# Unpadded attention tiles, two weight conversions before the first tile's outputs, and the sign cast of sixteen blocks on GpSimd

## The chip, the core and the metric

The kernel runs on one core of a Trainium2 chip. The metric is device microseconds (us) of one execution; the number quoted is a median of three. Engines: TensorE (PE; its weight loads are PEld), VectorE (DVE), ScalarE (ACT), GpSimd (POOL), and SyncE (SP), which here only issues transfers. Each engine works through its own instructions in the order in which the program gives them.

## What is computed

A recurrent attention of batch 4, 8 heads, 768 positions and head size 48 is followed by two feed-forward layers with gates:

```
y[t]  = r[t] @ (state + u * k[t] v[t]^T);   state = w * state + k[t] v[t]^T
h     = max(x @ w1, x @ w2, x @ w3);        x2 = h @ w_out
xn    = rms_norm(x2) * g
out   = (silu(xn @ w_gate) * (xn @ w_val)) @ w_out2
```

x has 3072 rows of 384; the first layer is 768 wide, the second 1536. All inputs are float32, and the products are made from a high and a low part of each operand (three matmuls for one).

## The kernel before

Attention. The 768 positions are cut into 6 chunks of 128, for 4 batches each: 24 tiles. For a tile i, `load_tile` (L251) queues four transfers on SP: two halves of `raw` (r and k transposed, 48 partitions each, L258), r and k as 128 rows (`tm`, L260), and v as 128 rows (L261). `raw` has three buffers of [128, 2, 514], `tm` three buffers whose parts r, k and v begin at elements 0, 386 and 770 (`KO`, `VO`); so the 514, 386 and 770 leave gaps of two elements behind rows of 512, 384 and 768. `load_next` issues one queued transfer. `prep` multiplies `raw` by powers of the decay (L316, DVE) and makes `ru` = r * u * k (L324, L325; DVE for the first eight tiles). `prep_b` sums `ru` by heads (L332, DVE) and puts the sums on diagonals, `Dg` (L335, POOL). `prep2` scales k (L343, POOL). `pe_a` makes the masked scores `pa` of a tile on PE (L352), `mix` merges them into `Dg` (L359, DVE), `pe_y` makes the outputs `py` (L410, PE), `fin` splits these into high and low x (L425 ACT, L426 DVE), and `pe_st` makes the state update (L378 PE, L365 ACT, and from the second chunk on L384 and L386 on POOL).

Weights. They arrive as 64-bit words and are converted into float32 in 60 blocks of 128x384, numbered by `jobs`: 0 to 17 for the first layer's three inputs, 18 to 23 for its output, the rest for the second layer. One `tick` (L221) advances a conversion pipeline by a step: with a counter i it issues the load of block i+3 (`conv_load`, L124, SP; five buffers `wraw`), the three ACT instructions of block i+1 (`conv_exp`: L137 scales the high word, L139 writes the 16 low bits of each element, L140 casts to float16 and so writes sign and exponent into the 16 high bits), the merge of block i on DVE (`conv_shift`, L147), and the split of block i-1 (`conv_put`, `w_split`: high part on ACT, L155; the low part, L156, is put off until after the next step of the program, on POOL, or on DVE for blocks 2, 16, 19 and 22).

Order. It is written out by hand. The part before the loop makes decay tables, loads tiles 0 to 2, does `prep` of tiles 0 and 1 and `pe_a(0)`, and calls `tick` twice, which only issues the loads of blocks 0 and 1. Then six steps are run one after another, each followed by the put-off work, one transfer and one `tick` (L619): `block(0)`, `ahead(2)`, `ahead_b(2)`, `block(1)`, `ahead(3)`, `ahead_b(3)`. `block(i)` is `pe_a(i+1)`, `mix(i+1)`, `pe_y(i)`, `fin(i)`, `pe_st(i)` and the queuing of tile i+3; `ahead` is `prep` with two transfers, `ahead_b` is `prep_b` and `prep2`. After that the first feed-forward layer runs in slots of nine matmuls (`a_l1`, L99 to L101, then L492, L495, L497 and L498 on ACT, DVE and POOL), with the remaining attention steps and the ticks (`U0T`) between the slots. The low part of the first layer's x and h goes to POOL where a slot has 256 columns. The first wide stretch of matmuls begins there; all of the second layer comes after 400 us.

Of the kernel before, what the change touches and what calls it, by code (L numbers as in the profile page):

```python
# [9 lines left out]
F32 = mybir.dt.float32  # L10
# [8 lines left out]
DRAM = bass.MemoryType.DRAM  # L19

B, H, S, D = 4, 8, 768, 48
KO = 386
VO = 770

# [2 lines left out]
RMS_EARLY = 2  # L29
WARM = 24  # L30
TKI = (0, 0, 2)
TKP = (1, 1, 1, 1, 1, 1)
HF = 2
U0T = (1, 1, 1, 1, 0, 1, 1, 1, 0, 1, 1, 1, 1, 1, 1, 0, 1, 1, 1, 0, 1, 1, 1, 1, 1, 1, 1, 1, 1, 1)
LEAD = 4

# [24 lines left out]
NP = H // 2  # L63
# [8 lines left out]
def rwkv_moe_kernel(ctx, tc, rkT, rkv, wd, ub, cst, rg, w1p, wo1p, w2p, out):  # L72
# [59 lines left out]
    def conv_exp(n):  # L132
        if n - 6 >= conv_put.job:
            sums_step(99)
        w = cw[n] = cp.tile([128, CW], F32, tag="wf", bufs=6, name=f"wf{n}")
        lo, hi = conv_words(n)
        act.activation(w, hi.bitcast(F32), AF.Copy, scale=2.0 ** -112)  # L137
        x = cbits(n).rearrange("p (n two) -> p n two", two=2)
        act.activation(x[:, :, 0], lo, AF.Copy, scale=2.0 ** -29 * (1 - 2.0 ** -12), bias=-0.4996)  # L139
        act.activation(x[:, :, 1].bitcast(F16), w, AF.Copy)  # L140

    def cbits(n):
        return craw[n].bitcast(U16)[:, 0:2 * CW]
# [77 lines left out]
    def tick(n=1):  # L221
        for _ in range(n):
            i = tick_n[0]
            tick_n[0] += 1
            for off, fn in ((3, conv_load), (1, conv_exp), (0, conv_shift), (-1, conv_put)):
                if 0 <= i + off < NJ:
                    fn(i + off)
# [10 lines left out]
    kt = tp.tile([128, DM], F32, name="kt")  # L238
    Tst = [tp.tile([128, NP, 96], F32, name=f"T{b}") for b in range(B)]

    raws = [tp.tile([128, 2, 514], F32, name=f"raw{n}") for n in range(3)]


    raw_t, tm_t, loads = {}, {}, []
# [1 line left out]
    def load_next(n=1):  # L246
        for _ in range(n):
            if loads:
                loads.pop(0)()

    def load_tile(i):  # L251
        if i >= NT:
            return
        a = raws[i % 3][:, :, 0:512].rearrange("p s (q t) -> p s q t", t=128)
        t = tp.tile([128, VO + NP * 144], F32, tag="tm", bufs=3, name=f"tm{i}")
        raw_t[i], tm_t[i] = a, t
        for j in range(2):
            loads.append(lambda j=j: sync.dma_start(a[64 * j:64 * j + 48], rkT[i, 48 * j:48 * j + 48]))  # L258
        rk = t[:, 0:2 * KO].rearrange("p (s n) -> p s n", s=2)[:, :, 0:DM]
        loads.append(lambda: sync.dma_start(rk, rkv[i, :, 0:2 * DM].rearrange("p (s n) -> p s n", s=2)))  # L260
        loads.append(lambda: sync.dma_start(t[:, VO:], rkv[i, :, 2 * DM:]))  # L261

    def tables():
        p = ap_.tile([128, NP, 65], F32, tag="h1h", name="ptab")
# [53 lines left out]
    def prep(i):  # L318
        prep_raw(i)
        s = st[i]  # L320
        tm = s["tm"]
        ru = tp.tile([128, DM], F32, tag="ru", name=f"ru{i}")
        eng = dve if i < NRU else pool
        eng.tensor_tensor(out=ru, in0=tm[:, 0:DM], in1=usb, op=ALU.mult)  # L324
        eng.tensor_tensor(out=ru, in0=ru, in1=tm[:, KO:KO + DM], op=ALU.mult)  # L325
        s["ru"] = ru

    def prep_b(i):
        s = st[i]
        a8 = tp.tile([128, H], F32, tag="a8", bufs=2, name=f"a8{i}")  # L330
        ru = s["ru"]
        dve.tensor_reduce(out=a8, in_=ru.rearrange("p (h d) -> p h d", d=D), op=ALU.add,  # L332
                          axis=mybir.AxisListType.X)
        Dg = tp.tile([128, H, 128], F32, tag="Dg", bufs=2, name=f"Dg{i}")
        pool.affine_select(out=Dg, in_=a8.unsqueeze(2).to_broadcast([128, H, 128]),  # L335
                           pattern=[[0, H], [1, 128]], channel_multiplier=-1, base=0,
                           compare_op=ALU.is_equal, fill=0.0)
        s["Dg"] = Dg

    def prep2(i):  # L340
        if i // B < NB - 1:
            k = st[i]["tm"][:, KO:KO + DM]
            pool.tensor_tensor(out=k, in0=k, in1=kt, op=ALU.mult)  # L343

    def pe_a(i):
# [9 lines left out]
    def mix(i):  # L355
        s = st[i]
        dg = s["Dg"].rearrange("p (r j) t -> p r j t", j=2)
        for j in range(2):
            dve.copy_predicated(out=dg[:, :, j], mask=cmask.unsqueeze(1).to_broadcast([128, NP, 128]),  # L359
                                data=s["pa"][j])  # L360
# [6 lines left out]
    def pe_st(i):  # L367
        s = st[i]
        c, b = divmod(i, B)
        if c == NB - 1:  # L370
            return
        tm = s["tm"]
        v3 = tm[:, VO:].rearrange("p (r q e) -> p r q e", q=3, e=D)
        pk = psx.tile([128, NP, D], F32, tag="x", name=f"pkv{i}")
        for pr in range(NP):
            for j in range(2):
                o = KO + 96 * pr + 48 * j
                pe.matmul(pk[64 * j:64 * j + 64, pr], tm[:, o:o + 64], v3[:, pr, 2 * j], start=True, stop=True)  # L378
        if c == 0:
            mask_kv(Tst[b], pk)  # L380
        else:
            kv = tp.tile([128, NP, 96], F32, tag="kv", name=f"kv{i}")
            mask_kv(kv, pk)
            pool.tensor_tensor(out=Tst[b], in0=Tst[b],  # L384
                               in1=w128.unsqueeze(2).to_broadcast([128, NP, 96]), op=ALU.mult)
            pool.tensor_tensor(out=Tst[b], in0=Tst[b], in1=kv, op=ALU.add)  # L386
# [190 lines left out]
    with tc.manual_schedule():  # L577
# [36 lines left out]
        prep(1)  # L614
        load_tile(2)
        load_next(4)
        prep_b(1)
        prep2(1)
        while pos < 6:  # L619
            steps[pos]()  # L620
            flush()
            pos += 1
            load_next()
            tick(TKP[pos - 1])

# [513 lines left out]
        def recurrence():  # L1139

            TB = 8
            wf = gp.tile([96, NP], F32, name="g_w")
            uf = gp.tile([96, NP], F32, name="g_u")
            m2 = gp.tile([96, 2], F32, name="g_m")
            sync.dma_start(wf, wd)
            sync.dma_start(uf, ub.rearrange("(r p) -> p r", p=96))
            sync.dma_start(m2, cst[0:96, 256:258])
            state = gp.tile([96, B, NP, D], F32, name="g_state")
            dve.memset(state, 0.0)

            def wide(a):
                return a.unsqueeze(1).unsqueeze(3).to_broadcast([96, B, NP, D])

            with tc.For_i(0, NB) as c, tc.For_i(0, 128, TB) as t0:
                rk = gp.tile([96, B, 2, NP, TB], F32, tag="g_rk", name="g_rk")
                for b in range(B):
                    for s in range(2):
                        sync.dma_start(rk[:, b, s], rkT[bass.ds(c * B + b, 1), :, s, :, bass.ds(t0, TB)].squeeze(0))
                py = psx.tile([D, B, NP, 2, TB], F32, tag="x", name="g_py")
                for t in range(TB):  # L1160
                    v = gp.tile([96, B, NP, D], F32, tag="g_v", bufs=3, name=f"g_v{t}")
                    for b in range(B):
                        row = rkv[bass.ds(c * B + b, 1), bass.ds(t0 + t, 1), 2 * DM:].rearrange(
                            "a o (r q e) -> (a o) r q e", q=3, e=D)
                        for j in range(2):
                            sync.dma_start(v[48 * j:48 * j + 48, b],
                                           row[0, :, 2 * j].partition_broadcast(48))
                    r, k = (rk[:, :, s, :, t:t + 1].to_broadcast([96, B, NP, D]) for s in range(2))
                    cur = gp.tile([96, B, NP, D], F32, tag="g_cur", bufs=2, name=f"g_cur{t}")
                    dve.tensor_tensor(out=v, in0=v, in1=k, op=ALU.mult)  # L1170
                    dve.tensor_tensor(out=cur, in0=v, in1=wide(uf), op=ALU.mult)
                    dve.tensor_tensor(out=cur, in0=cur, in1=state, op=ALU.add)
                    dve.tensor_tensor(out=cur, in0=cur, in1=r, op=ALU.mult)
                    dve.tensor_tensor(out=state, in0=state, in1=wide(wf), op=ALU.mult)
                    dve.tensor_tensor(out=state, in0=state, in1=v, op=ALU.add)
                    for b in range(B):
                        for pr in range(NP):
                            pe.matmul(py[:, b, pr, :, t], cur[:, b, pr], m2, start=True, stop=True)
                ys = gp.tile([D, B, NP, 2, TB], F32, tag="g_ys", bufs=2, name="g_ys")
                act.copy(ys, py)  # L1180
                for b in range(B):
                    dst = yd[bass.ds(c, 1), :, b, bass.ds(t0, TB)].squeeze(0)
                    sync.dma_start(dst.rearrange("(r e) t -> e r t", e=D),
                                   ys[:, b].rearrange("e r j t -> e (r j) t"))
# [128 lines left out]
```

## Time and profile before

| what | us |
|---|---|
| median of 3 runs (814.71 to 815.89) | 815.61 |
| the profiled execution | 816.15 |
| its span, first to last instruction | 814.4 |
| PE busy in the span | 793.0 |
| DVE, ACT, POOL busy | 578.6, 427.3, 241.1 |

The profiled execution is 0.54 us above the median, and 1.75 us of it lie around the span. PE is busy for 97% of the span. A row of the timeline reads: start in us, duration in us, engine, line, operation, tile written from tiles read, sizes, count; in brackets the idle time of the engine ahead of it and what ended that. "issue" stands for a wait that the profile can't name.

### The profile page before, as it was taken

Reading aid. Unit: us, or ns where it says so; the run is one execution under the profiler, and the core shown is the slowest. Engines: PE = TensorE matmul, PEld = TensorE weight load, DVE = VectorE, ACT = ScalarE, POOL = GpSimd, SP = SyncE. Lnnn points to the kernel's source line nnn. Section 1 sums busy time; section 2 is a strip of 40 time slices with the busy share of each in tenths; the row PEclk is TensorE's granted clock in tenths of the full one; section 3 lists DMA queues with packets and bytes.
Section 4 is the critical chain, followed back from the end, with each engine's and each line's share of the span. In section 5 each row is a group of like instructions: output and inputs, shape, how many; then the busy total and the mean of one; then the engine's idle time right before and its main releaser. Section 6 shows DMA issues by size and latency. Waiting matters only on the chain.

```text
span 814.4 us, 14091 instructions
## 1 busy us (share of the span) xinstructions
PE 793.0 (97%) x5098; PEld 652.2 (80%) x5098; DVE 578.6 (71%) x948; ACT 427.3 (52%) x812; POOL 241.1 (30%) x241
## 2 busy tenths in 40 slices
PE   7799999999999999999999999999999999999996
PEld 6688887888888888888787888788888788888884
DVE  8898979948959748518946679866677884665551
ACT  1998865455453542224576666555444555444431
POOL 2488834544354541013267773000000000000000
PEclk8999999999999999999999999999999999999999
DMA  9996685666475654035279874318454405544211
GB/s 240 272 271 187 222 251 179 187 218 206 136 236 160 211 188 147 20 130 165 87 247 331 282 238 169 118 57 278 139 183 145 130 26 175 157 153 141 73 40 43
DMA packets 83594, 139.28 MB, mean 171 GB/s; under 512 B 10550, under 2 KB 46902, under 8 KB 83516
## 3 DMA queue, kind: packets, MB, share of 16 engines
q1 hardware_dynamic: 80172, 122.37, 48.9%
q0 software_dynamic: 3200, 15.73, 5.1%
q8 instruction: 42, 0.69, 0.4%
q14 instruction: 36, 0.29, 0.1%
q10 hardware_dynamic: 144, 0.20, 0.1%
HBM read 98.65 MB, written 35.41 MB: 165 GB/s over the span
## 4 chain that ended last, share of the span: by engine, by line
PE 84%; DVE 6%; DMA 3%; ACT 3%; issue 2%; SPq 0%; POOL 0%; DVEq 0%; ACTq 0%; POOLq 0%
PE px L99 11%; PE px L100 11%; PE px L101 11%; PE pl L99 8%; PE pl L101 7%; PE pl L100 7%; PE pa L100 5%; PE pa L101 5%; PE pa L99 5%; PE py L410 4%; PE po L100 3%; PE po L99 3%; PE po L101 3%; PE pa L352 2%; DMA raw<-in_rkT 1%
## 5 line engine op out<-in xcount | busy, mean ns | idle before, releaser
L99 PE MATMUL pl<-x,w_a 128*128 128x512 f32 (+1 forms) x342 | 132.0, 386 | 1.4 <-DVE c L495 1.0
L100 PE MATMUL pl<-x,w_a 128*128 128x512 f32 (+1 forms) x342 | 129.6, 379 | 0.7 <-DVE x L426 0.7
L101 PE MATMUL pl<-x,w_a 128*128 128x512 f32 (+1 forms) x342 | 129.6, 379 | 0.5 <-POOL w_a L156 0.5
L99 PEld LDWEIGHTS pl<-x,w_a 128*128 128x128 f32 x342 | 64.3, 188 | 15.0 <-DVE c L495 1.4
L101 PEld LDWEIGHTS pl<-x,w_a 128*128 128x128 f32 x342 | 64.3, 188 | 13.0 <-POOL w_a L156 0.7
L100 PEld LDWEIGHTS pl<-x,w_a 128*128 128x128 f32 x342 | 64.4, 188 | 12.6 <-DVE x L426 1.1
L495 DVE TENSOR_TENSOR c<-pl,c 128x512 f32<-128x512 f32 (+1 forms) x76 | 49.9, 657 | 28.8 <-PE pl L101 26.6
L1031 DVE TENSOR_TENSOR px<-px,sb 128x512 f32<-128x512 f32 x56 | 39.0, 698 | 33.0 <-PE px L101 32.1
L497 ACT CAST h1h<-c 128x512 fp32r<-128x512 f32 (+1 forms) x32 | 19.0, 594 | 82.1 <-DVE c L495 82.0
L147 DVE SCALAR_TENSOR_TENSOR wf<-wf,wraw 128x384 uint32<-128x384 uint32 x60 | 46.3, 775 | 13.1 <-ACT wraw L140 12.6
L335 POOL TENSOR_SCALAR_AFFINE_SELECT Dg<-a 128x1024 f32<-128x1024 f32 x24 | 30.2, 1259 | 80.2 <-DVE a L332 67.2
L1019 ACT COPY sb<-px 128x512 f32<-128x512 f32 x63 | 37.0, 587 | 32.0 <-PE px L101 28.3
L657 POOL TENSOR_TENSOR ws<-wsf,ws 128x384 fp32r<-128x384 f32 x40 | 41.7, 1042 | 40.1 <-ACT ws L656 29.9
L100 PE MATMUL px<-hb,wo 128*128 128x512 f32 x132 | 51.6, 391 | 0.2 <-DVE hb L1017 0.2
L99 PE MATMUL px<-hb,wo 128*128 128x512 f32 x132 | 51.6, 391 | 0.0
L101 PE MATMUL px<-hb,wo 128*128 128x512 f32 x132 | 51.4, 390 | 0.0
L359 DVE COPY_PREDICATED Dg<-csb,pa 128x512 f32<-128x512 uint32 x48 | 32.5, 731 | 20.3 <-PE pa L352 17.1
L410 PE MATMUL py<-Dg,tm 128*32 128x128 f32 x768 | 40.6, 288 | 0.0
L1055 DVE TENSOR_TENSOR hb<-h,hb 128x512 fp32r<-128x512 f32 x36 | 24.9, 691 | 21.8 <-ACT hb L1054 21.6
L139 ACT ACTIVATE wraw<-wraw 128x384 uint16<-128x384 uint32 x60 | 38.9, 648 | 2.0
L140 ACT ACTIVATE wraw<-wf 128x384 f16<-128x384 f32 x60 | 38.7, 645 | 2.0
L137 ACT ACTIVATE wf<-wraw 128x384 f32<-128x384 f32 x60 | 33.5, 558 | 11.2 <-DMA w2o<-wf 10.1
(306 smaller groups left out, 2116.5 us busy)
## 6 DMA issues: line engine op xcount, KB each, us to landing
ws<-w2s SPq DMA_DIRECT2D x80, 384.0 KB, 3.0
w2s<-ws POOLq DMA_DIRECT2D x40, 384.0 KB, 3.5
wraw<-in_w2p SPq DMA_DIRECT2D x36, 384.0 KB, 5.1
raw<-in_rkT SPq DMA_DIRECT2D x48, 192.0 KB, 3.6
tm<-in_rkv SPq DMA_DIRECT2D x24, 384.0 KB, 4.1
wsf<-w2f SPq DMA_DIRECT2D x120, 64.0 KB, 3.2
tm<-in_rkv SPq DMA_DIRECT2D x24, 288.0 KB, 4.4
wraw<-in_w1p SPq DMA_DIRECT2D x18, 384.0 KB, 7.9
```

The costliest lines, as they stand in the source:

```text
L99: pe.matmul(o, lh, rh, start=start, stop=False, **kw)
L100: pe.matmul(o, lh, rl, start=False, stop=False, **kw)
L101: pe.matmul(o, ll, rh, start=False, stop=stop, **kw)
L137: act.activation(w, hi.bitcast(F32), AF.Copy, scale=2.0 ** -112)
L139: act.activation(x[:, :, 0], lo, AF.Copy, scale=2.0 ** -29 * (1 - 2.0 ** -12), bias=-0.4996)
L140: act.activation(x[:, :, 1].bitcast(F16), w, AF.Copy)
L147: dve.scalar_tensor_tensor(out=wu, in0=wu, scalar=3, in1=cbits(n).bitcast(U32), op0=ALU.logical_shift_left, op1=ALU.bitwise_or)
L410: pe.matmul(o, l, r, start=start, stop=stop)
L495: dve.tensor_tensor(out=c1[:, :n], in0=p[:, :n], in1=c1[:, :n], op=ALU.max)
L657: pool.tensor_tensor(out=t[:, :, 1], in0=r, in1=r32(t[:, :, 0]), op=ALU.subtract)
L1019: (act.copy if kind == "e" else dve.tensor_copy)(get(ks[1]), get(ks[0]))
L1031: dve.tensor_tensor(out=o, in0=a, in1=b, op=op)
```

## The change

The tiles lose their gaps: `raw` becomes [128, 2, 4, 128], the parts of `tm` begin at 0, 384 and 768, and r and k come as one row of 768 elements instead of two of 384. Two ticks are moved up: the first stands behind the loads of tile 2, the second behind `mix(1)`, with `block(0)` written out around it; the ticks of the loop then begin with `ahead(2)`. From there on every tick does a block one higher than before at the same place in the program. For blocks 2 to 17 the cast to float16 is issued on POOL instead of ACT.

```diff
-KO = 386
-VO = 770
+VO = 768
-TKP = (1, 1, 1, 1, 1, 1)
+TKP = (0, 1, 1, 1, 1, 1)
+POOL_S = tuple(range(2, 18))
...
-        act.activation(x[:, :, 1].bitcast(F16), w, AF.Copy)
+        if n in POOL_S:
+            pool.tensor_copy(x[:, :, 1].bitcast(F16), w)
+        else:
+            act.activation(x[:, :, 1].bitcast(F16), w, AF.Copy)
...
-    raws = [tp.tile([128, 2, 514], F32, name=f"raw{n}") for n in range(3)]
+    raws = [tp.tile([128, 2, NP, 128], F32, name=f"raw{n}") for n in range(3)]
...
-        a = raws[i % 3][:, :, 0:512].rearrange("p s (q t) -> p s q t", t=128)
+        a = raws[i % 3]
...
-        rk = t[:, 0:2 * KO].rearrange("p (s n) -> p s n", s=2)[:, :, 0:DM]
-        loads.append(lambda: sync.dma_start(rk, rkv[i, :, 0:2 * DM].rearrange("p (s n) -> p s n", s=2)))
-        loads.append(lambda: sync.dma_start(t[:, VO:], rkv[i, :, 2 * DM:]))
+        loads.append(lambda: sync.dma_start(t[:, 0:VO], rkv[i, :, 0:VO]))
+        loads.append(lambda: sync.dma_start(t[:, VO:], rkv[i, :, VO:]))
...
         prep(1)
         load_tile(2)
         load_next(4)
+        tick()
         prep_b(1)
         prep2(1)
+        pe_a(1)
+        mix(1)
+        tick()
+        pe_y(0)
+        fin(0)
+        pe_st(0)
+        load_tile(3)
+        pos = 1
+        load_next()
         while pos < 6:
```

The other lines replace `KO` by `DM` where k is read.

## Rows read from the trace of the kernel before

**Rows 1.** Windows: length, busy us (count) of PE, PEld, DVE, ACT, POOL; clock, DMA
```profile
20.00:40.00 20.00, 15.63 (x213) 13.31 (x216) 17.13 (x27) 18.91 (x39) 8.76 (x8) 0.91 1.00 270
40.00:60.00 20.00, 18.36 (x215) 16.59 (x208) 18.19 (x28) 19.33 (x42) 16.97 (x15) 1.00 0.93 266
60.00:80.00 20.00, 20.00 (x230) 16.58 (x230) 17.55 (x27) 16.24 (x34) 16.17 (x15) 1.00 0.65 198
```

**Rows 2.** Timeline of PE: starts of the tiles' scores, and the wait near 128 us
```profile
29.76 1.25 PE L352 MATMUL pa<-raw 48*128 48x128 f32 x16 [0.49 <-PE pl L101]
...
38.39 1.25 PE L352 MATMUL pa<-raw 48*128 48x128 f32 x16 [1.14 <-issue]
...
49.43 1.25 PE L352 MATMUL pa<-raw 48*128 48x128 f32 x16 [1.03 <-issue]
...
60.84 1.16 PE L352 MATMUL pa<-raw 48*128 48x128 f32 x16
...
73.01 1.16 PE L352 MATMUL pa<-raw 48*128 48x128 f32 x16
...
128.53 0.50 PE L99 MATMUL pl<-x,w_a 128*128 128x512 f32 x1 [0.98 <-DVE c L495]
```

**Rows 3.** Timeline of ACT: first output, a wait for a load, one sign cast
```profile
20.05 0.48 ACT L425 CAST x<-py 128x384 fp32r<-128x384 f32 x1 [5.83 <-PE py L410]
...
28.41 0.56 ACT L137 ACTIVATE wf<-wraw 128x384 f32<-128x384 f32 x1 [0.39 <-DMA wraw<-in_w1p]
...
48.51 0.63 ACT L140 ACTIVATE wraw<-wf 128x384 f16<-128x384 f32 x1
```

**Rows 4.** Timeline of SP and the transfers' sums of 0 to 70 us
```profile
20.70 0.38 SPq L260 DMA_DIRECT2D tm<-in_rkv  x1
...
22.31 0.91 SPq L124 DMA_DIRECT2D wraw<-in_w1p  x2
...
q1 hardware_dynamic: 9042, 17.41, 90.2%
```

**Rows 5.** Timeline of DVE: products of raw, ru, merges, and two waits for ACT
```profile
28.44 1.21 DVE L316 TENSOR_TENSOR raw<-raw,qk 128x1024 f32<-128x1024 f32 x1
...
32.87 0.64 DVE L156 TENSOR_TENSOR w_a<-wf,w_a 128x384 fp32r<-128x384 f32 x1 [1.22 <-ACT w_a L155]
...
39.96 0.55 DVE L147 SCALAR_TENSOR_TENSOR wf<-wf,wraw 128x384 uint32<-128x384 uint32 x1
...
47.28 2.04 DVE L316 TENSOR_TENSOR raw<-raw,qk 128x1024 f32<-128x1024 f32 x1
...
56.96 1.53 DVE L316 TENSOR_TENSOR raw<-raw,qk 128x1024 f32<-128x1024 f32 x1
...
64.77 0.79 DVE L147 SCALAR_TENSOR_TENSOR wf<-wf,wraw 128x384 uint32<-128x384 uint32 x1 [1.41 <-ACT wraw L140]
...
69.77 1.25 DVE L316 TENSOR_TENSOR raw<-raw,qk 128x1024 f32<-128x1024 f32 x1
```

**Rows 6.** Timeline of POOL: a one-input operation, and operations of two inputs
```profile
0.99 0.10 POOL L265 MEMSET ptab<- 128x4 f32 x1
...
17.51 1.09 POOL L335 TENSOR_SCALAR_AFFINE_SELECT Dg<-a 128x1024 f32<-128x1024 f32 x1 [1.67 <-DVE a L332]
...
46.98 1.26 POOL L156 TENSOR_TENSOR w_a<-wf,w_a 128x384 fp32r<-128x384 f32 x1 [1.36 <-ACT w_a L155]
48.21 1.71 POOL L498 TENSOR_TENSOR h1l<-c,h1h 128x256 fp32r<-128x256 f32 x1
...
52.03 1.01 POOL L156 TENSOR_TENSOR w_a<-wf,w_a 128x384 fp32r<-128x384 f32 x1 [0.83 <-ACT w_a L155]
```

**Rows 7.** Window from 28.10 to 49.40 us, columns as in rows 1
```profile
28.10:49.40 21.30, 17.51 (x208) 15.61 (x209) 18.92 (x29) 20.25 (x42) 12.82 (x13) 1.00 1.05 281
```

More of the change, by code (lines that the diff above doesn't have):

```diff
@@ L324, in prep @@
         eng.tensor_tensor(out=ru, in0=tm[:, 0:DM], in1=usb, op=ALU.mult)
-        eng.tensor_tensor(out=ru, in0=ru, in1=tm[:, KO:KO + DM], op=ALU.mult)
+        eng.tensor_tensor(out=ru, in0=ru, in1=tm[:, DM:2 * DM], op=ALU.mult)
         s["ru"] = ru
@@ L341, in prep2 @@
         if i // B < NB - 1:
-            k = st[i]["tm"][:, KO:KO + DM]
+            k = st[i]["tm"][:, DM:2 * DM]
             pool.tensor_tensor(out=k, in0=k, in1=kt, op=ALU.mult)
@@ L376, in pe_st @@
             for j in range(2):
-                o = KO + 96 * pr + 48 * j
+                o = DM + 96 * pr + 48 * j
                 pe.matmul(pk[64 * j:64 * j + 64, pr], tm[:, o:o + 64], v3[:, pr, 2 * j], start=True, stop=True)
@@ L1162, in recurrence @@
                     for b in range(B):
-                        row = rkv[bass.ds(c * B + b, 1), bass.ds(t0 + t, 1), 2 * DM:].rearrange(
+                        row = rkv[bass.ds(c * B + b, 1), bass.ds(t0 + t, 1), VO:].rearrange(
                             "a o (r q e) -> (a o) r q e", q=3, e=D)
```

## The prediction, made before the changed kernel ran

> **What bounds the kernel now.** I read the busy times in windows first. From 60 us on PE is busy in every us of a window [rows 1], so a time lost or won ahead of that stays in the total unless PE waits later. The timeline of PE then has only one wait of weight left before 400 us, 0.98 us at 128.53 [rows 2]. So the change is decided between 20 and 60 us. There PE is busy for 15.63 and 18.36 us of 20, ACT for 18.91 and 19.33, DVE for 17.13 and 18.19, while POOL rises from 8.76 to 16.97 [rows 1]. ACT is nearly full, and its conversions also follow their loads: block 3's began 0.39 us after ACT was free, when its words landed [rows 3]. The transfers are full as well, with a share of 0.93 to 1.00 [rows 1].
>
> PE's waits show who is last. The scores of tiles 3, 4 and 5 start at 29.76, 38.39 and 49.43 us after waits of 0.49, 1.14 and 1.03 us [rows 2]. In DVE's timeline the product `raw` of tile 3 runs from 28.44 for 1.21 us and that of tile 5 from 47.28 for 2.04, so it ends at 49.32, 0.11 us ahead of the scores that wait for it [rows 5]. Tile 6's ends at 58.49 and its scores start at 60.84; tile 7's end at 71.02 and start at 73.01 [rows 2, 5]. PE hangs on DVE without slack until tile 5, and has 2.35 and 1.99 us of slack after.
>
> Why does that product take 2.04 us when 1.21 is its usual time? POOL had a low part from 46.98 to 48.24; 48.24 plus 1.08 is 49.32. POOL's next operation was issued at 48.21 and took 1.71, to 49.92, although its work is shorter than a plain low part of 1.01 [rows 6]. The rows read as one operation holding the other off for its whole length: a DVE instruction with two inputs from SBUF and a POOL instruction take turns. I count the two as one resource.
>
> **The change part by part.**
>
> *The cast on POOL.* ACT loses sixteen casts of 0.63 us each, 10.1 us [rows 3]; POOL gets sixteen. No row shows that cast on POOL. From below: the diagonal select reads one input, takes 1.09 us for 1024 elements, and the least a POOL operation takes is 0.10 [rows 6]; 384 elements at that rate are 0.99 x 384 / 1024 + 0.10 = 0.47 us. From above: the low part, two inputs of the same 384 elements, 1.01 us. A cast has one input, which puts it near 0.47, but it also writes 2-byte elements with a step; I take 0.65. Nothing in the rows makes it a gain on POOL itself.
>
> By a page the price would be a little lower: the Trainium skill, "GPSIMD Engine Reference", section 3.1, gives 1.8 cycles for an element as the best case of a plain loop at 1.2 GHz, an estimate of 0.58 us for 384. No run here shows it yet; by it the sum below would be 0.8 us smaller.
>
> What POOL has free where it counts: from 28.10 to 49.40 it is busy for 12.82 of 21.30 us, idle for 8.48 [rows 7]. In that idle time DVE runs seven two-input operations, two products of 1.21 us, three `ru` and two merges of 0.54 to 0.56, from 28.44 to 39.96 [rows 5], 5.2 us in all. The shared resource is free for 8.5 - 5.2 = 3.3 us. The change puts into the stretch the casts of blocks 3 to 10, 8 x 0.65 = 5.2 us, and, since every tick is one block ahead, one more low part of 1.0 us: 6.2 us. So 6.2 - 3.3 = 2.9 us don't fit, and tile 5's product ends 2.9 us later; PE has no slack there and is 2.9 us late. With 0.47 us it is 3.8 + 1.0 - 3.3 = 1.5, with 1.02 it is 5.9.
>
> From tile 5 to tile 6 come casts 11 to 14, 2.6 us against 2.35 of slack, 0.25 more; to tile 7 casts 15 to 17, 1.95 us against 1.99, nothing more. At 1.02 us a cast the two would add 1.7 and 1.1. Off that go two waits of DVE for ACT, 1.22 us at 32.87 and 1.41 at 64.77 [rows 5]; I leave them out at 0.65, where the count is of the shared resource and not of DVE, and subtract them at the upper end: 5.9 + 1.7 + 1.1 - 2.6 = 6.1.
>
> *The new order of waiting.* The merge of block i on DVE now waits for POOL, where it waited for ACT. Behind the merge in DVE's queue stand the next tile's product and the outputs' low part, so PE waits for them. Ahead of the cast in POOL's queue stand a low part, and twice a select and the scaling of k. This is why I count no free time twice.
>
> *Two ticks earlier.* ACT is idle for 5.83 us ahead of the first outputs at 20.05 [rows 3]; blocks 0 and 1 cost it two scalings, two writes and two casts of some 0.6 us, 3.7 us at most, which fit. DVE's first merge stands between `mix(1)` and the outputs' low part, where DVE waits for ACT anyway. On SP the loads of blocks 2 and 3 pass tile 3's: block 3's was issued at 22.31, behind a `tm` load of tile 3 that waited for its buffer until 20.70 [rows 4], and now goes out ahead of it. ACT's wait of 0.39 us at 28.41 goes. Tile 3's `raw` is not needed on DVE before 28.44. Gain on the path: nothing by 29.76, since the scores of tile 3 wait for DVE; 0.5 us before it is lost again there. If those loads came so late that ACT were still casting at 20.05, the price would be that delay.
>
> *No gaps.* A tile's transfers shrink from 192 + 256 + 128 packets to 96 + 128 + 128, 224 fewer. On the main queue 9042 packets took 90.2% of 16 x 70 us [rows 4], 112 ns each; if all of a packet's time were fixed, that is 224 x 112 / 16 = 1.6 us of transfer a tile, and if all went by bytes, nothing. A single larger packet may hold up another load by its own length, some 0.1 us. I take nothing on the path: the loads of the next blocks already go ahead of their need with the new order, and the shared resource is what is late.
>
> The Trainium skill, "DMA: Bandwidth & Descriptors", section "Why small descriptors are slow", speaks against much from this part: a packet has about 3 cycles of overhead on 32-byte beats, so 48 beats for 1536 B carry 6%, and merging two saves half of it. By it a tile's transfer is 3% shorter, where my upper end is far more; no row separates the two.
>
> *Later.* The wait of 0.98 us at 128.53 [rows 2] is for DVE, which is behind ACT and sums there. The conversions are one ahead, so their sums start one slot earlier, and PE arrives later; I take 0.5 us back, between 0 and 0.98.
>
> **Sum.** 2.9 + 0.25 - 0.5 = +2.65 us on the profiled execution of 816.15 gives 818.8; that execution stands 0.54 above the median of the runs, so 818.3. The ends of the cast's price give +0.5 (1.5 - 0.98) and +6.1, medians of 816.1 and 821.7.
>
> **The rivals.** *Relief reaches PE (faster).* ACT and the loads, not the shared resource, are what holds DVE between 28 and 49 us, and the casts slip into what is free. For it: ACT is busy for 20.25 of 21.30 us, the loads' share is 1.05 [rows 7], POOL's low parts wait for ACT for 1.36 and 0.83 us [rows 6]. Against: DVE itself is busy for 18.92 us there. Its idle time, 2.4 us, is the most that PE can win, and with 0.5 us at 128.53 the profile would take 813.3, the median 812.7. It decides where a cast costs under 0.29 us of the shared resource (3.3 us less one low part, over eight casts), which it may if part of a cast's length needs nothing shared. Chance 0.15.
>
> *Absorbed (no change).* Waits for ACT that end (2.6 us) pay for the casts (2.9 us): 815.6 within 1.6. Chance 0.25.
>
> *Queues in step (slower still).* Each merge waits for its cast, and the low part queued behind the cast runs first: up to 1.0 us a tick for some five ticks, beyond the count above. It would give the upper end, about 821.5, and so would a cast of 1.0. Chance 0.15.
>
> *The merge of rows does nothing,* or the rows stay in two packets: no term of mine changes.
>
> **How the numbers follow.** The forecast has 0.45, the heavier case 0.15, no change 0.25, faster 0.15. What this measurement can tell from no change is 0.2%, 1.6 us. Slower 0.60, same 0.25, faster 0.15. The range of 8 in 10 goes from the faster case, 812.7, to the upper end, 821.8; given slower alone it is 817.2 to 821.8.
>
> **What would show it.** POOL's new row of 128x384 f16 near 0.65 us, and hardly an idle us on POOL from 34 to 66; merges and products of DVE that last longer and waits of DVE for POOL in place of those for ACT; ACT well below 19 us in the window from 40 to 60; the scores of tile 5 near 52 us instead of 49.43, and the steps from there to tile 7 unchanged. The forecast is wrong if these scores start before 49.4, if the cast is under 0.3 us, or if PE waits after 60 us for something new.

## The result, and the profile after

The changed kernel takes 825.13 us (822.87 to 825.61) against 815.55 (814.48 to 815.89) for the kernel before on the same chip: 1.0115 times as long, 95% interval 1.0099 to 1.013. That is slower, as forecast, but by 9.4 us where the forecast had 2.7, and outside the range.

The windows after, with columns as in [rows 1], and one window more, around the later wait:

```profile
20.00:40.00 20.00, 15.64 (x174) 13.09 (x173) 16.51 (x25) 13.02 (x29) 12.40 (x15) 0.73 0.93 258
40.00:60.00 20.00, 16.48 (x210) 14.71 (x209) 17.56 (x25) 12.42 (x29) 18.43 (x18) 0.91 0.64 192
60.00:80.00 20.00, 19.77 (x175) 16.66 (x175) 16.87 (x23) 13.61 (x30) 18.34 (x20) 1.00 0.81 247
120.00:140.00 20.00, 17.30 (x142) 13.70 (x141) 18.99 (x37) 12.06 (x27) 9.65 (x10) 0.91 0.75 236
```

From 40 to 60 us ACT went from 19.33 us of 20 to 12.42. Nothing was gained by it: DVE is a little less busy than before, and PE lost 1.9 us. The third number from the right, the granted clock, is 0.73 and 0.91 where [rows 1] has 0.91 and 1.00; after 120 it is 0.91 again, where the kernel before has 1.00:

```profile
120.00:140.00 20.00, 19.02 (x218) 15.02 (x216) 19.29 (x35) 10.22 (x20) 9.32 (x8) 1.00 0.55 169
```

PE's timeline after, the rows that answer to [rows 2] (scores of tiles 3 to 7, then the wait near 128):

```profile
31.83 2.17 PE L354 MATMUL pa<-raw 48*128 48x128 f32 x16 [2.37 <-issue]
41.53 1.25 PE L354 MATMUL pa<-raw 48*128 48x128 f32 x16 [0.38 <-PE pl L101]
54.06 1.79 PE L354 MATMUL pa<-raw 48*128 48x128 f32 x16 [1.78 <-issue]
67.11 1.16 PE L354 MATMUL pa<-raw 48*128 48x128 f32 x16
79.57 1.25 PE L354 MATMUL pa<-raw 48*128 48x128 f32 x16 [0.23 <-PE pl L101]
...
128.85 0.50 PE L99 MATMUL pl<-x,w_a 128*128 128x512 f32 x1 [2.70 <-DVE c L497]
129.19 0.39 PE L100 MATMUL pl<-x,w_a 128*128 128x512 f32 x1
...
129.99 0.63 PE L100 MATMUL pl<-x,w_a 128*128 128x512 f32 x1
```

Tile 5 is 4.6 us late, tile 6 is 6.3. The waits of 2.37 and 1.78 us are for `raw`, as before, only longer, and the wait of 0.98 near 128 has become 2.70. Behind each of these three, matmuls run at the lower of the clock's two levels: the scores take 2.17 us where 1.25 is usual, and a matmul of the first layer 0.63 where 0.39 was usual right before.

Why `raw` is late stands in DVE's timeline and POOL's, here ahead of tile 5 (L150 is the merge, L318 the product; L141 the cast, L159 a low part, L500 the low part of `h1`):

```profile
48.77 0.87 DVE L150 SCALAR_TENSOR_TENSOR wf<-wf,wraw 128x384 uint32<-128x384 uint32 x1
...
51.12 1.33 DVE L150 SCALAR_TENSOR_TENSOR wf<-wf,wraw 128x384 uint32<-128x384 uint32 x1 [0.62 <-POOL wraw L141]
52.38 1.58 DVE L318 TENSOR_TENSOR raw<-raw,qk 128x1024 f32<-128x1024 f32 x1
```

```profile
49.18 1.33 POOL L159 TENSOR_TENSOR w_a<-wf,w_a 128x384 fp32r<-128x384 f32 x1
50.46 0.63 POOL L141 CAST wraw<-wf 128x384 f16<-128x384 f32 x1
51.01 1.02 POOL L159 TENSOR_TENSOR w_a<-wf,w_a 128x384 fp32r<-128x384 f32 x1
52.20 0.72 POOL L141 CAST wraw<-wf 128x384 f16<-128x384 f32 x1 [0.16 <-POOL w_a L159]
```

DVE waits 0.62 us at the merge, until the cast ends at 51.09. By then the low part queued behind the cast has begun, at 51.01, and the merge, which takes 0.55 us alone, takes 1.33: 52.03, the low part's end, plus 0.42. So one tick costs DVE 0.62 + 0.78 us, and the product is queued behind. DVE's waits from 20 to 100 us (line waited at, releaser: us in all, times, longest) list the merge's waits for the cast five times:

```profile
DVE wf L150 <- POOL wraw L141: 5.1, 5, 2.5
DVE Dg L361 <- POOL Dg L337: 4.0, 5, 1.0
```

Two more of the five stand ahead of tile 5; the longest one comes only after the scores of tile 6:

```profile
28.92 1.32 DVE L150 SCALAR_TENSOR_TENSOR wf<-wf,wraw 128x384 uint32<-128x384 uint32 x1 [0.72 <-POOL wraw L141]
...
38.53 1.33 DVE L150 SCALAR_TENSOR_TENSOR wf<-wf,wraw 128x384 uint32<-128x384 uint32 x1 [0.72 <-POOL wraw L141]
...
72.53 1.05 DVE L150 SCALAR_TENSOR_TENSOR wf<-wf,wraw 128x384 uint32<-128x384 uint32 x1 [2.55 <-POOL wraw L141]
```

The three ahead of tile 5 are 2.06 us of waiting and 2.33 us of longer merges, 4.4 of the 4.6 us by which tile 5 is late. The one of 2.55 us is of another kind: its cast stood behind a select and a scaling of k in POOL's queue, which ran from 69.53 to 71.93. This is the mechanism that the prediction kept as a rival, "Queues in step". The runs below say how much of the 9.4 us it is.

### The profile page after: what moved, and what is told of

The parts are those of the page before. It is cut to its first block, busy times and chain, and to the rows that moved or that the text cites. A ratio compares the mean times of both kernels' runs of the same rounds, so it can differ in the third digit from the quotient of the medians.

```text
span 823.4 us, 14096 instructions
## 1 busy us (share of the span) xinstructions
PE 798.3 (97%) x5098; PEld 657.4 (80%) x5098; DVE 583.3 (71%) x948; ACT 419.6 (51%) x796; POOL 258.9 (31%) x257
## 2 busy tenths in 40 slices
DMA packets 78218, 139.28 MB, mean 169 GB/s; under 512 B 10550, under 2 KB 40758, under 8 KB 78140
## 4 chain that ended last, share of the span: by engine, by line
PE 81%; DVE 8%; POOL 3%; issue 3%; ACT 2%; DMA 2%; SPq 0%; DVEq 0%; POOLq 0%; ACTq 0%
PE px L99 10%; PE px L100 10%; PE px L101 10%; PE pl L99 7%; PE pl L100 7%; PE pl L101 7%; PE pa L100 5%; PE pa L101 5%; PE pa L99 5%; PE py L412 3%; PE po L101 2%; PE po L100 2%; PE po L99 2%; PE pa L354 2%; DVE wf L150 1%
## 5 line engine op out<-in xcount | busy, mean ns | idle before, releaser
L150 DVE SCALAR_TENSOR_TENSOR wf<-wf,wraw 128x384 uint32<-128x384 uint32 x60 | 51.0, 852 | 9.8 <-POOL wraw L141 5.1
L412 PE MATMUL py<-Dg,tm 128*32 128x128 f32 x768 | 43.0, 299 | 0.0
L354 PEld LDWEIGHTS pa<-raw 48*128 48x128 f32 x384 | 26.5, 204 | 15.8 <-issue 11.9
L354 PE MATMUL pa<-raw 48*128 48x128 f32 x384 | 31.3, 302 | 8.1 <-issue 5.8
```

Of the source, the lines that this page charges most:

```text
L150: dve.scalar_tensor_tensor(out=wu, in0=wu, scalar=3, in1=cbits(n).bitcast(U32), op0=ALU.logical_shift_left, op1=ALU.bitwise_or)
L354: pe.matmul(pa[j][:, pr], raw[sl, 1, pr], raw[sl, 0, pr], start=True, stop=True)
L412: pe.matmul(o, l, r, start=start, stop=stop)
```

## The experiments

Each was timed beside the kernel before on the same chip; 0.1% is 0.8 us. Two ratios whose intervals overlap widely are not shown to differ. "Largest wait" is PE's between 85 and 140 us.

| kernel | ratio to before, 95% | tile 5, tile 6 scores at | largest wait |
|---|---|---|---|
| before | 1 | 49.43, 60.84 | 0.98 at 128.5 |
| after | 1.0115 (1.0099 to 1.013) | 54.06, 67.11 | 2.70 at 128.9 |
| a2 cast alone | 1.0053 (1.0039 to 1.0068) | 51.67, 63.06 | 1.34 at 124.2 |
| a4 ticks alone | 1.0026 (1.0012 to 1.004) | 49.05, 60.45 | 3.09 at 122.1 |
| a3 rows alone | 1.0013 (1.0003 to 1.0024) | 50.05, 61.45 | 1.41 at 129.7 |
| a1 rows and ticks | 1.0043 (1.0029 to 1.0057) | 51.83, 63.23 | 3.32 at 125.1 |
| c1 after, merge a tick later | 1.0069 (1.0053 to 1.0085) | 50.56, 62.13 | 3.02 at 89.7 |
| f2 after, cast a tick earlier | 1.0087 (1.007 to 1.0105) | 52.53, 63.84 | 3.28 at 127.3 |
| c2 after, one tick less | 1.0074 (1.0058 to 1.009) | 54.03, 65.43 | 1.40 at 135.1 |
| c4 after, waits filled | 1.0098 (1.0079 to 1.0117) | 54.92, 66.22 | 1.78 at 128.0 |
| d1 c1 and c2 together | 1.006 (1.0046 to 1.0074) | 50.77, 62.37 | 1.41 at 132.9 |
| c3 ticks, one less | 0.9986 (0.9974 to 0.9998) | 49.88, 61.28 | 0.41 at 128.4 |
| d4 c3 and cast, merge later | 1.0035 (1.0023 to 1.0047) | 50.20, 61.64 | 1.15 at 122.8 |
| e1 d4, cast to block 12 | 1.0027 (1.0015 to 1.0038) | 50.65, 62.93 | 1.00 at 131.2 |
| f1 c3 and cast, cast earlier | 1.0038 (1.0025 to 1.005) | 51.49, 62.87 | 1.10 at 131.7 |
| e4 c3 and rows | 1.000 (0.999 to 1.001) | 50.42, 63.43 | 0.47 at 130.6 |
| e2 before, one tick less | 1.0013 (1.0 to 1.0026) | 49.19, 60.59 | 2.14 at 103.2 |
| e3 c3, two ticks less | 0.9977 (0.9966 to 0.9987) | 50.25, 61.67 | under 0.4 |
| d3 c3, waits filled | 1.002 (1.0011 to 1.003) | 49.10, 60.49 | 1.11 at 128.4 |
| d2 a3, first buffer with gaps | 1.0015 (1.0006 to 1.0024) | 49.99, 61.40 | 1.43 at 129.5 |

### The three parts, one by one

**a1, rows and ticks:** the changed kernel with the cast left on ScalarE.

```diff
-POOL_S = tuple(range(2, 18))
+POOL_S = ()
```

> The changed kernel with all sign casts back on ACT: rows without gaps and the two earlier ticks alone. Theory 1 (the casts on POOL make VectorE wait, PE then waits and its clock falls): no wait of DVE for a cast on POOL; the scores of tile 3, 4, 5 at 29.5, 38 and 48.5 us instead of 31.83, 41.53 and 54.06, granted clock 1.0 from 30 us on, total 813 to 816. Rival 2 (the earlier ticks put one more conversion into a full stretch and are the loss): total 820 or more. Rival 3 (larger packets hold up the loads): total above 818, ACT or DVE waiting for loads.

**a2, the cast alone:** the kernel before with the line `pool.tensor_copy(...)` for blocks 2 to 17.

> The kernel before with only the sign casts of blocks 2 to 17 on POOL, gaps kept, no earlier ticks. Theory 1: 821 to 826, scores of tile 5 at 53 us or later, granted clock under 0.8 somewhere between 30 and 60 us. Rival 2 and rival 3 (the loss is in the ticks or the rows): within 2 us of 815.6.

**a3, the rows alone:** the kernel before with the tiles' rows as after, nothing else.

> The kernel before with only the rows without gaps. Theory 1: within 1.6 us of 815.6, the loads' packets 9 % fewer. Rival 3: 818 or more. If the loads were what holds ACT back between 28 and 45 us: 813 to 814.

**a4, the ticks alone:** the kernel before with the new order of steps and `TKP = (0, 1, 1, 1, 1, 1)`.

> The kernel before with only the two earlier ticks. Theory 1: within 2 us of 815.6, ACT's wait for the words of block 3 gone, conversions of blocks 0 and 1 between 14 and 19 us. Rival 2: 819 or more, with a longer wait of PE near 128 us than 0.98.

All three parts cost: 0.53%, 0.26% and 0.13%, together 0.92% of the 1.15%; the rest is interaction. That the cast by itself explains the loss is refuted. Alone, the cast made tile 5 2.2 us late and tile 6 too. That is near the forecast's 2.9, but 1.4 of it is one merge that waits for its cast (0.62 us) and then takes 0.77 longer:

```profile
48.74 1.32 DVE L151 SCALAR_TENSOR_TENSOR wf<-wf,wraw 128x384 uint32<-128x384 uint32 x1 [0.62 <-POOL wraw L142]
```

The ticks did by tile 6 what they are for, 0.4 us ahead of before, and lost far more at 122. a4's PE row there, and DVE's queue ahead of it:

```profile
122.10 0.50 PE L99 MATMUL pl<-x,w_a 128*128 128x512 f32 x1 [3.09 <-DVE c L495]
```

```profile
113.02 0.56 DVE L147 SCALAR_TENSOR_TENSOR wf<-wf,wraw 128x384 uint32<-128x384 uint32 x1 [4.16 <-ACT wraw L140]
...
118.47 0.55 DVE L147 SCALAR_TENSOR_TENSOR wf<-wf,wraw 128x384 uint32<-128x384 uint32 x1
...
119.26 0.97 DVE L168 TENSOR_TENSOR wf<-wf,wf 128x128 f32<-128x128 f32 x1
120.16 1.08 DVE L168 TENSOR_TENSOR wx<-wx,wf 128x128 f32<-128x128 f32 x1
...
121.36 0.68 DVE L495 TENSOR_TENSOR c<-pl,c 128x512 f32<-128x512 f32 x1
```

PE waits for the max (L495). Ahead of it DVE stood for 4.16 us at a merge whose conversion waited on ACT, 2.17 us for the sums of the second layer and 1.88 for their store to leave the buffer:

```profile
106.38 0.56 ACT L137 ACTIVATE wf<-wraw 128x384 f32<-128x384 f32 x1 [2.17 <-DVE wf L168]
...
111.08 0.56 ACT L137 ACTIVATE wf<-wraw 128x384 f32<-128x384 f32 x1 [1.88 <-DMA w2f<-wf]
```

A converter that is one block ahead meets the second layer's sums and stores, for which the same buffers are needed, one slot earlier, and blocks two queues there.

### The lead, taken back

**c2, c3:** the changed kernel, and the kernel with the ticks alone, with one tick fewer behind tile 6; e4 is c2 without the cast.

```diff
-U0T = (1, 1, 1, 1, 0, 1, 1, 1, 0, 1, 1, 1, 1, 1, 1, 0, ...
+U0T = (1, 1, 1, 1, 0, 1, 1, 1, 0, 1, 1, 1, 0, 1, 1, 0, ...
```

> The changed kernel with one tick of the converter fewer after the tile 6 stretch (the 13th entry of U0T is 0), so that from there on the conversions stand where they stood in the kernel before. Theory Lead (the early ticks are paid at the wait near 128, because the second layer's sums come one tick earlier and stand in VectorE's queue ahead of the max that PE waits for): the wait of 2.70 us at 128.9 falls to 1 or less, PE's granted clock stays at 1.0 there, tile 6's scores stay at 67.1 within 0.5, and the median falls by 2.5 to 3.5 us, to 821.5 to 822.5. Rival (the wait at 128.9 only follows from the later product): the wait stays above 2 us and the median within 1 of 825.

> The kernel before with the two conversions ahead of the first tile's outputs alone, and one tick fewer after the tile 6 stretch (the 13th entry of U0T is 0). Theory Lead: tile 6's scores start near 60.45, 0.4 ahead of the kernel before, the wait at 122 falls from 3.09 to about 1, the clock stays at 1.0, and the median is 0.3 to 1.5 us below the kernel before. Rival (the wait follows from something else that the early ticks shift): the median stays 1 to 3 us above the kernel before.

> The changed kernel with the cast left on ScalarE and one tick fewer later: rows and early ticks, the lead taken back. Theory Rows cost 1 us: median at 815.5 to 816.3, about 1.1 above the same kernel with gaps in the rows (814.84). Rival (rows cost nothing that lasts): median at 814.4 to 815.2.

The lead is shown as the price of the ticks: one entry gave back 0.41% of the changed kernel, 3.3 us, the clock behind the wait too, and turned the ticks alone from 1.0026 to 0.9986. The wait of 2.70 fell to 1.17 and 1.40, a little above what was expected; and tile 6 came at 65.43 instead of 67.1, since the clock didn't fall behind tile 5 in this run. So 1.7 of the 3.6 us between the two profiles lie ahead of the tick that was taken out, and aren't its doing. The two other pairs have no such head start (tile 6 comes 0.8 us later in c3 than in a4, 0.2 later in e4 than in a1) and give 0.40% and 0.43%, 3.3 and 3.5 us.

**e2, e3:** the same entry alone in the kernel before; and c3 with the 25th entry of `U0T` set to 0 as well.

> The kernel before with one tick of the converter fewer after the tile 6 stretch and nothing else (the 13th entry of U0T is 0). Theory Lead as a scale (each tick that the converter stands further back at 100 us takes load off the wait near 128): the wait of 0.98 at 128.5 shrinks to under 0.5 and the median falls by 0.3 to 1 us. Theory Early (the early conversions bring the gain, by 0.4 at tile 6, and the tick less only takes back their price): the median of this kernel is within 0.3 of before or above it.

> The kernel before with the two early conversions and two ticks fewer later (the 13th and the 25th entry of U0T are 0), so the converter stands one block behind the kernel before from about 100 us on. Theory Lead as a scale: the wait at 128 goes wholly and the median falls a little under 814.84, by up to 0.7 us. Rival (with one tick less the balance is reached; a conversion later than before is missed by the second layer's stores): median at 815 to 817.

The entry alone doesn't help. The wait near 128 goes, but PE then waits for output weights that came too late:

```profile
103.16 0.50 PE L101 MATMUL po<-h1h,w_o 128*128 128x512 f32 x1 [2.14 <-POOL w_o L156]
```

So the blocks before 100 us have to be early, and those after it late: early ticks with one fewer behind them do both. With two fewer no wait of 0.4 us is left between 85 and 140, and e3 has the lowest ratio of the study, 0.9977 (0.9966 to 0.9987), 814.34 us beside 815.69; the intervals don't separate it from c3.

### The wait at the merge

**c1:** in the changed kernel, merge and put of blocks 2 to 17 one tick later, so that the cast has a tick's time.

```diff
-for off, fn in ((3, conv_load), (1, conv_exp), (0, conv_shift), (-1, conv_put)):
+for off, fn in ((3, conv_load), (1, conv_exp)):
 ...
+for fn, at in ((conv_shift, i), (conv_put, i - 1)):
+    for n in (at - 1, at):
+        if 0 <= n < NJ and n == at - (n in POOL_S):
+            fn(n)
```

> The changed kernel, but for blocks 2 to 17 the merge on VectorE (conv_shift) and the put behind it stand one tick later in the program, so the cast on GpSimd has a whole tick to finish before VectorE comes to the merge. All arithmetic is done. Theory Order (VectorE, in order, waits at the merge for the cast, and raw of tile 5 is late by that): the five waits of the merge for the cast, 5.1 us together, go to near nothing, tile 5's scores start near 51.8 as they do with the cast left on ScalarE, and the median falls from 825 to 819 to 821. Theory Turns (VectorE and GpSimd take turns whatever the order): the waits go but the instructions of both stay stretched, tile 5's scores stay within 0.7 of 54.1 and the median within 1.5 of 825.

**f2:** in the changed kernel, load, first conversions and cast of these blocks one tick earlier instead; merge and put stand where they stood.

```diff
-for off, fn in ((3, conv_load), (1, conv_exp), (0, conv_shift), (-1, conv_put)):
+for off, fn in ((3, conv_load), (1, conv_exp)):
+    for n in (i + off, i + off + 1):
+        if 0 <= n < NJ and n == i + off + (n in POOL_S):
+            fn(n)
+for off, fn in ((0, conv_shift), (-1, conv_put)):
 ...
```

> The changed kernel with the load, the two conversions on ScalarE and the cast of blocks 2 to 17 one tick earlier, merge and put where they stand, and the lead at 128 not taken back. Theory Order: the merge's waits of 5.1 us go, tile 5's scores start near 50.5 and tile 6's near 62, and the median falls to 818.5 to 820, that of the change with the cast left on ScalarE (819.32). Theory Turns: tile 6's scores at 62 to 63, the median at 821 to 823.

DVE's waits in c1 have the merge's wait at 0.5 us in place of 5.1, and tile 5's scores start at 50.56, 3.5 us before those of the changed kernel:

```profile
DVE Dg L365 <- POOL Dg L341: 5.2, 5, 2.2
DVE c L501 <- PE pl L101: 1.1, 1, 1.1
DVE wf L150 <- POOL wraw L141: 0.5, 1, 0.5
```

That the order made tile 5 late is thereby shown for 3.5 of its 4.6 us. But c1 won 0.46% and f2 0.28%, 3.8 and 2.3 us, and neither reached a1, where the cast is on ScalarE. In c1 a wait took the place of the one removed:

```profile
89.68 1.62 PE L358 MATMUL pa<-raw 48*128 48x128 f32 x11 [3.02 <-issue]
```

**d1** has both undoings.

> The changed kernel with both undoings at once: the merge and the put of blocks 2 to 17 one tick later, and one tick fewer after the tile 6 stretch. If the two prices are separate (the merge's wait ahead of tile 6, the lead at the wait near 128), their gains add: 825 - 4.2 - 3.5 = 817 to 818, tile 6's scores near 62.1, and no wait of PE above 1.5 us after 100. Rival (the late merge has put a wait of its own at 89.7, 3.0 us with the clock falling behind it, so that part of its gain went back): the wait at 89 stays above 2 us, the median lies at 818.5 to 821.

The gains didn't add: 1.006 is 1.1 us below c2 and 0.7 below c1, both within the intervals. The wait at 89.7 is gone, and others stand at 104.4 (1.39 us, for `h1l`) and 132.9.

### What the cast costs without that wait

**d4, f1, e1** put the cast into c3, where neither rows nor lead disturb: with the merge one tick later (d4), with the cast one tick earlier (f1), and as d4 for blocks 2 to 12 alone (e1).

> The kernel before with the two early conversions, one tick fewer later, and the cast of blocks 2 to 17 on GpSimd with the merge and the put one tick later: the change without its rows and with both undoings. Theory Order holds all of the cast's price: without VectorE's wait at the merge, tile 6's scores lie within 1 us of 61.3 and the median within 1 us of the same kernel without the cast (814.84). Theory Turns has a share: GpSimd's work stretches VectorE's, tile 6's scores come 1 to 2 us late, 62.3 to 63.3, and the median lies at 816 to 818.

> The kernel before with the two early conversions, one tick fewer later, and the cast of blocks 2 to 17 on GpSimd, with the load, the two conversions on ScalarE and the cast of these blocks one tick earlier and the merge and the put where they stand. Theory Order (the wait at the merge and the put's lateness are the price): no wait of the merge for the cast, no wait at 103, tile 6's scores near 61.3, median 814 to 815.8. Theory Turns (the casts' own time on GpSimd makes the rest of GpSimd's and VectorE's work later): median 817 to 818.5, as with the merge one tick later.

> The kernel before with the two early conversions, one tick fewer later, and the cast on GpSimd with the later merge for blocks 2 to 12 only; blocks 13 to 17 are cast on ScalarE as before. Theory Full (what is left of the cast's price comes from 60 to 80 us, where GpSimd was busy 19.58 of 20 us with the casts of blocks 13 to 17 in it): GpSimd's busy time in that stretch falls to 16 to 17.5, the wait of 1.0 at 103 goes, and the median lies within 0.8 of 814.84. Rival (the cast costs where it stands, by the shared turns, also early): the median stays at 817 to 818.

Against c3's 0.9986 the cast costs 0.49% in d4 and 0.52% in f1, 4.0 and 4.2 us, without a wait at the merge and by two different edits. "Order holds all of the price" falls. Nor is it paid at tile 5, where the forecast had it: the products of tile 5 in c3, d4 and f1, in this order, end at 49.78, 50.11 and 50.22 us.

```profile
47.73 2.05 DVE L316 TENSOR_TENSOR raw<-raw,qk 128x1024 f32<-128x1024 f32 x1
```

```profile
48.51 1.60 DVE L324 TENSOR_TENSOR raw<-raw,qk 128x1024 f32<-128x1024 f32 x1
```

```profile
48.63 1.59 DVE L324 TENSOR_TENSOR raw<-raw,qk 128x1024 f32<-128x1024 f32 x1
```

From 26 to 50 us DVE is busy for 22.84 us in d4 and 20.95 in c3, 1.9 more, and c3's waits of DVE for ACT there, 1.9 us, are gone. Up to tile 5 the ended waits paid for the casts. d4 is still only 0.4 us behind c3 at tile 7 (73.90 against 73.46), and 4.0 at tile 12, behind waits of PE of 1.02, 1.15 and 1.11 us at 103, 123 and 132. The windows from 40 to 60 and 60 to 80 us, of c3, then of f1:

```profile
40.00:60.00 20.00, 19.64 (x230) 17.94 (x229) 18.23 (x27) 19.09 (x42) 16.57 (x16) 0.93 0.88 258
60.00:80.00 20.00, 20.00 (x230) 16.58 (x230) 17.34 (x27) 15.55 (x33) 14.93 (x15) 1.00 0.57 181
```

```profile
40.00:60.00 20.00, 18.06 (x215) 16.58 (x215) 16.68 (x26) 14.29 (x33) 20.00 (x21) 0.91 0.82 241
60.00:80.00 20.00, 20.00 (x230) 16.58 (x230) 17.97 (x24) 9.72 (x21) 17.22 (x16) 1.00 0.56 170
```

POOL (fifth busy time) is busy for all 20.00 us from 40 to 60, and ACT, which the change was to relieve, for 9.72 of 20 from 60 to 80: ACT now waits for the others. With POOL full, its selects come late too. In f1 DVE stands 5.8 us in all for the diagonal (3.0 in c3), 2.16 us ahead of tile 6 alone:

```profile
57.14 1.38 DVE L367 COPY_PREDICATED Dg<-csb,pa 128x512 f32<-128x512 uint32 x2 [2.16 <-POOL Dg L343]
```

Of f1's 4.2 us, 1.6 are lost by tile 6 (62.87 against 61.28); 1.5 more show at 122 and 132, where PE waits 0.79 and 1.10 us for the max, against 0.41 in c3. e1 freed POOL from 60 to 80 us (15.00 us busy, 19.58 in d4) and removed the wait at 103, both as expected by "Full", yet its ratio fell by 0.08% only; its tile 7 has become late instead (75.66 against 73.90 in d4). So what the late casts cost by themselves, and whether POOL without free time is the cause, stays open.

### Clock and rows

**c4, d3:** matmuls of the all-ones tile ahead of scores that wait, in the changed kernel and in c3 (there also ahead of the first transposes).

```diff
+for _ in range(FILL.get(i, 0)):
+    pe.matmul(pa[0][:, 0], r32(ones), r32(ones), start=True, stop=True)
```

> The changed kernel with matmuls of the all-ones tile ahead of the scores of tile 3 (14 of 128x128), 4 (4) and 5 (12), written into the bank that the scores then overwrite: TensorE works on in its waits for raw. All arithmetic of the reference is done. Theory Clock (part of the loss is that TensorE falls to the lower level, 1.2 GHz, around the waits at 31.8 and 54.1): the half-clock stretches 30.8 to 37.6 and 54.7 to 58.1 go or shrink to under 2 us together, tile 4's scores start 1 to 2 us earlier than 41.5, tile 6's near 65, and the median falls by 1.5 to 3 us to 822 to 823.5. Rival (raw is what is late, the clock is only where PE had slack): the clock comes back but tile 4's, 5's and 6's scores stay within 0.5 of 41.5, 54.1 and 67.1 and the median within 1 of 825.

> The kernel before with the two early conversions, one tick fewer later, and matmuls of the all-ones tile in TensorE's waits: 8 ahead of the transposes at 13, 6 ahead of the scores of tile 1, 12 of tile 2, 6 of tile 4. Nothing of the reference is left out. Theory Clock matters early: the half-clock stretches at 12.1, 22.3 and 39.4 go, the products of the first tiles run at 1.2 to 1.5 us in place of 2.2 to 2.8, tile 6's scores start 0.5 to 1.5 us before 61.3, and the median falls to 813 to 814.3. Rival (up to tile 6 the raw product on VectorE sets the pace and a faster TensorE only waits longer): clock back, tile 6's scores within 0.4 of 61.3, median within 0.6 of the same kernel without the filling (814.84).

c4's windows from 20 to 60 show the clock at 0.89 and 1.00 where the changed kernel had 0.73 and 0.91:

```profile
20.00:40.00 20.00, 18.08 (x218) 15.97 (x216) 16.51 (x25) 14.11 (x31) 13.30 (x15) 0.89 0.91 249
40.00:60.00 20.00, 17.12 (x233) 15.77 (x233) 17.56 (x24) 11.52 (x27) 18.44 (x18) 1.00 0.64 201
```

c4's ratio is 0.17% below the changed kernel's, 1.4 us, and the two intervals overlap too far to call that a gain. Tile 4's scores stayed at 41.51 and tile 5's came 0.9 us later, behind their filling: up to tile 5 the clock only runs where PE has to wait anyway. Where c4's profile is ahead is behind 54 us, with tile 6 0.9 us earlier, and at 128, where the wait is 1.78 instead of 2.70. In d3 tile 6 came 0.8 us earlier than in c3, but the wait at 128.4 grew from 0.41 to 1.11, tile 12's scores start at 151.0 in both, and the kernel is 2.8 us (0.34%) slower. That loss lies behind 151; 1.02 us of it is a wait for ACT near 428 that c3 has not. Why it came is open. In neither kernel was filling a gain that the runs show.

**d2:** rows merged, but the first of the three `raw` buffers keeps its gap.

> The kernel before with the tiles loaded without gaps in their rows, except that the first of the three raw buffers keeps its gap (tiles 0, 3, 6 and so on: 2 KB pieces, and the longer issue). Theory Small load (the rows cost only at the start: raw and tm of tile 0 reach the DMA queues earlier and in larger pieces, and the 0.8 KB load of the decay, on which VectorE's first product waits, lands later, 4.1 us after its issue in place of 3.1): the landing goes back below 3.5 us, VectorE's first clamp starts before 4.7 (5.47 with all rows merged, 4.43 before), and tile 1's scores start before 15.5. The median lies 0.5 to 1 us under that of all rows merged, within 0.1% of the kernel before. Rival (chance of the landing, or tm's pieces): the landing stays at 3.8 or above and the clamp after 4.9.

The rows cost 0.13%, 0.17% and 0.14% (a3 to before, a1 to a4, e4 to c3), 1.1 to 1.4 us each time, where the forecast had nothing; only a3's is clear of noise by itself. One place shows: `raw` of tile 0 is issued in 0.78 us instead of 1.35, and its larger packets run beside the 0.8 KB load of the decay, on which DVE's first product waits. That load's median landing in a3 (last column, us):

```profile
small<-in_wd SPq DMA_DIRECT2D x2, 0.8 KB, 4.1
```

It is 3.1 in the kernel before, 2.9 to 3.3 in the ten profiles with gaps and 3.1 to 4.1 in the nine with merged rows. In the nine runs with merged rows DVE began that work at 4.57 to 5.47 us, 4.91 on the mean; in the ten at 4.25 to 4.73, 4.48 on the mean. d2 brought the landing back to 3.2 and the start to 4.58, but not the time (1.0015). So the load is late as described, and it isn't shown to be what costs 1.1 us. That stays open.

## Why the prediction was wrong

**The cast's price was right.** Taken at 0.65 us; POOL's sixteen rows in the changed kernel have 0.61 to 0.65 where DVE doesn't hold them off, and up to 1.14 where it does, 0.64 at the median. Where the merge doesn't wait for them the median is 0.95 (c1, f2, d4, f1). The figure worked out from the Trainium skill, "GPSIMD Engine Reference", section 3.1 (0.58, an estimate) was lower than every row.

**The step that failed first: the count for tile 5.** It had 6.2 us of POOL work for 3.3 us of shared free time, and so tile 5's product 2.9 us late. With the same casts and no wait at the merge, the product ends 0.3 and 0.4 us after c3's (d4, f1), and in c1 1.1 after that of the kernel before. At 0.65 us a cast it left out that DVE's waits for ACT end; up to tile 5 these paid for the casts (1.9 us in d4), as the rival "Absorbed" had it. That the forecast's 52 us for tile 5 lies near the cast alone (51.67) is luck: 1.4 of that run's 2.2 us come from one merge that waited.

**What stood in its place: the order.** "Queues in step" was a rival at 0.15, and the sum had nothing for it. Three merges ahead of tile 5 that waited and were then stretched are 4.4 of its 4.6 us, and c1 and f2 put the share of all five in the total at 2.3 to 3.8 us. An in-order engine that waits for a busy neighbour loses the wait and then meets the neighbour's next instruction. The rival's own number didn't follow either: up to 1.0 us for five ticks beyond the count is up to 823.3, not 821.5, and lies outside the range.

**What the casts cost behind tile 7 had no term.** The count ended there with "nothing more". Without a wait at the merge the cast still costs some 4 us, and in the profiles d4 loses 3.5 us between tiles 7 and 12, f1 1.8. Why is open.

**The step that failed most in sign: the wait at 128.** I took 0.5 us back, "their sums start one slot earlier". They do, and therefore stand ahead of the max that PE waits for: 2.70 us in place of 0.98, with the lower clock behind it, 3.3 to 3.5 us by the pairs a4 to c3 and a1 to e4. The bounds, 0 to 0.98 of gain, left the loss out without a reason.

**A term that was missing: the clock.** Three waits of PE were followed by stretches at 1.2 GHz. [Rows 1] showed 0.91 in the first window already. By itself it isn't shown to cost time: keeping it up in c4 made a difference of 1.4 us, within the noise. At tile 6, c2 came 1.7 us ahead of the changed kernel by it.

**The ticks and rows ahead of tile 6.** Nothing by 29.76, as I said: a4's tile 3 starts at 29.96, its tile 6 0.4 us ahead. For the rows I took nothing and they cost 1.1 or more. The packets fell by 5376, 24 tiles of 224, to 78218 in all, and no time came of it: my upper end of 1.6 us a tile was far off. The Trainium skill, "DMA: Bandwidth & Descriptors", section "Why small descriptors are slow", by which merged rows would be some 3% shorter (an estimate, for the rows of 1536 B alone), is nearer to that; no run here shows the 3%.

**The range.** Its upper end, 821.8, was the end of one unknown, the cast's. The ends of the others were all at or below zero, so it could not hold a case in which three parts lose at once.

In one sum against before, by the ratios of a chain of three steps: the cast 0.72% in the presence of the others (after against a1), of which c1 and f2 give 0.46% and 0.28% to the wait at the merge, and the rest stays open; the lead 0.43% (a1 against e4); and nothing for what is left (e4 against before, 1.000), where the rows' 0.14% stand against the 0.14% that the early ticks win behind a lead taken back (c3): 5.9 + 3.5 + 0 = 9.4 us. Another order of the steps would share out the interaction differently.

## What to carry to other kernels

Where work moves to an engine that feeds an in-order queue, write down the consumer's queue at that point: what waits there, what the producer runs next, and who stands behind; an average of free time says nothing of it. A stage that runs earlier isn't free either: look for the next place where its products need the same buffers, and shift it back there (here one entry of a schedule was worth 3.3 us). And relieving an engine gained nothing here, where the engine that took the work had no time to spare.

## What the runs showed of the hardware

A merge on DVE takes 0.55 us alone and 1.33 us when a low part of POOL has just begun; the cast on POOL 0.61 to 0.65 alone, up to 1.14 beside DVE in the changed kernel and up to 1.61 in a2. The rows read as the two holding each other off for whole instructions, in both directions, also with a cast of one input on POOL's side.

Around most waits of PE of 1.8 to 3.3 us the granted clock fell to its lower level, and the same scores took 2.17 us instead of 1.25. The changed kernel's wait of 1.78 us ahead of tile 5 had such a fall behind it, c2's of 1.77 in the same place had none, so two kernels that are the same up to there differed by 1.7 us at tile 6 (67.11 and 65.43).

A load of 0.8 KB landed 2.9 to 3.3 us after its issue in ten profiles with 2 KB pieces beside it, and 3.1 to 4.1 in nine with 4 KB pieces whose issue took 0.78 us in place of 1.35.
